# Three more tiles of a channel attention and feed-forward kernel in 16-bit pairs, with stores and scale lines on GpSimd's queue and VectorE's list ordered by due period

## The chip, the cores and the metric

The kernel runs on one core of a Trainium2 chip. The metric is the device time of one execution in microseconds (us), the median of three runs. A core has TensorE (PE; its weight loads are a row of their own, PEld), VectorE (DVE), ScalarE (ACT), GpSimd (POOL) and SyncE (SP), whose queue issues nearly all DMAs here.

## The reference

```python
B, N, C = (4, 6080, 256); d_ff = 2048
qn = q / (norm(q, axis=1) + 1e-6);  kn = k / (norm(k, axis=1) + 1e-6)
s = kn.transpose(0, 2, 1) @ qn / tau            # B x 256 x 256
a = softmax(s, axis=-1)
x = (v @ a).reshape(24320, 256)
h = x @ w_in
g = maximum(0.01 * h, h)
return g @ w_out
```

q, k and v are 32-bit; w_in and w_out arrive as 64-bit floats.

## The kernel before

The attention matrix of a batch is folded into the first weights: for batch b the kernel makes W'[b] = a[b] @ w_in (256 x 2048), and then every token needs only leaky(v @ W') @ w_out. Products are made from pairs: a number is a high and a low part, and high x high, low x high and high x low are added up (`PASSES`). The parts are fp32r (32 bits) in the first batch and 16-bit floats, scaled by powers of two, in the later ones. `T16` is the number of the first tile in 16-bit pairs.

A batch has NT = 6 tiles of tokens, four of 2 x 512 and two of 2 x 496 columns, so there are 24 tiles. A tile takes NPAIR = 8 steps, here called periods, numbered through the run: the fourth tile is periods 24 to 31. In a period TensorE makes the four blocks of h for a pair of feature blocks from seven block products of three matmuls (`block_product`, Strassen's scheme in Winograd's form), and 24 matmuls of the second layer for the period before (`ffn_out`, drawn in portions by `out(n)`). That is 45 matmuls of 512 or 496 columns a period, 360 a tile. Around them ScalarE copies out of PSUM (`taken`) and applies the leaky function (`leaky`), VectorE adds (`add`, three a period) and makes the low halves (the end of `leaky`, four a period).

Everything else hides beside these matmuls, in order of hand-made lists. `at(w, fn)` runs `fn` when period w is built; `put(queue, length, fn)` appends work to a list; at fixed places of each period `slot(queue, room)` takes work from the list's head while it is ready and its nominal lengths fit the room. On VectorE the rooms are 1.45, 2.2, 1.45 and 0.8 us a period from the second tile on. In the first batch that work is: the squares of batch 1's q and k (`square_work`: 47 ScalarE squares with 47 VectorE adds), the sums of w_in's blocks that W' needs (`sums_work`), the splits of the next tile of v (`v_parts`, `v_split_of`), the conversion of w_out into 16-bit pairs (`wo_half`), then the softmax of batch 1 and its W' (`norm_work`, `w_pair`, `w_parts`).

A `Scale` finds the power of two for a 16-bit split: `see` keeps each partition's largest value, `gather` takes their maximum and sends it to a line of DRAM, `read` brings the line back to all partitions, `find` computes the factors. There is one for W', one for w_out and one for each tile of v in 16 bits. All tiles share the SBUF tile `zeros` as the landing place.

W' of a batch lies in DRAM (`w_dram`); `w_load(i, p)` loads a pair's 14 blocks three periods ahead of use into one of four buffers, 896 KB as fp32r and 448 KB as 16-bit. SP's queue issues these loads, the loads of v, q and k, all stores and the lines of scales, in program order.

Of the kernel before, what the change touches and what calls it, by code (L numbers as in the profile page):

```python
# [18 lines left out]
P = 128  # L19
# [17 lines left out]
def channel_attention_ffn(  # L37
# [37 lines left out]
    T16 = NT  # L75
# [51 lines left out]

    class Scale:
# [3 lines left out]
        def __init__(self, name, parts, bufs=1):  # L132
            t = small.tile([P, 16], F32, name=name, bufs=bufs)
            self.most = t[:, 0:parts]
            self.top, self.e, self.up, self.down, self.out = (t[:, x:x + 1] for x in range(8, 13))
            self.line = dram.tile([P, 1], F32, name=name + "_line", bufs=bufs)
            self.seen = 0
# [13 lines left out]
        def read(self):  # L151
            self.all = zeros
            nc.sync.dma_start(out=self.all, in_=self.line.rearrange("p o -> (p o)").partition_broadcast(P))

        def find(self):
            e = self.e.bitcast(I32)
            nc.vector.tensor_reduce(out=self.e, in_=self.all, axis=AX.X, op=ALU.max)
            nc.vector.tensor_scalar(out=e, in0=e, scalar1=0x7F800000, scalar2=None, op0=ALU.bitwise_and)
# [9 lines left out]
            )  # L168

# [3 lines left out]
    class Scores:  # L173


        def __init__(self, b, sizes):
# [5 lines left out]
            self.raw, self.split = {}, {}  # L182
# [4 lines left out]
        def load(self, i, raw):  # L187
# [16 lines left out]
            return last  # L204

# [317 lines left out]

    def win_block(j, h, early):
# [4 lines left out]
        def store():  # L529
            w = win[j, h] = win_new[j, h]  # L530
            stores.append(lambda: nc.sync.dma_start(out=win_dram[j][h], in_=flat(w)))
            if j > 1:
                stores.pop()()
# [13 lines left out]
    def w_tile(i):  # L547
        return work.tile([P, 2, NS, P], pair_type(i), name="w_split", bufs=4)

# [22 lines left out]
    now, w_done, w_stores = [0], {}, []  # L572
# [5 lines left out]
    def w_parts(b, j):  # L578
# [34 lines left out]
        for k in range(2):  # L613
# [9 lines left out]
            def store(x0, n, w=w, p=p):  # L623
                if b:
                    nc.sync.dma_start(
# [12 lines left out]
            def rest(k=k, p=p, blocks=blocks, store=store):  # L638
# [3 lines left out]
                if b == 0:  # L642
                    w = w_split[0, p]
                    w_stores.append(lambda: nc.sync.dma_start(
# [7 lines left out]
    def w_load(i, p):  # L652
        assert (i // NT, p) in w_done
        w = w_tile(i)
        nc.sync.dma_start(
            out=f32(w.rearrange("p x s f -> p (x s f)")), in_=w_dram[i // NT, p].rearrange("p x f -> p (x f)")
        )
# [8 lines left out]

    def wo_region(n):
        return wo[0][:, n * FPB:(n + 1) * FPB, :].rearrange("p f d -> p (f d)")

    def wo_half(n):  # L670

        t, o = None, None
        hi, lo = (wo[x][:, n * FPB:(n + 1) * FPB, :].rearrange("p f d -> p (f d)") for x in range(2))

        def whole():
            nonlocal t, o
            t, o = temp(name="wo_whole"), temp(name="wo16").bitcast(F16)
            return nc.vector.tensor_tensor(out=t, in0=f32(hi), in1=f32(lo), op=ALU.add)

        def low():  # L680
# [3 lines left out]
            nc.sync.dma_start(out=wo16_dram[n], in_=o)  # L684
# [3 lines left out]
        return [  # L688
            ("dve", 0.7, whole),
            ("act", 0.75, lambda: nc.scalar.activation(out=o[:, 0:FPB * C], in_=t, func=AF.Copy, scale=wo_scale.up)),  # L690
            ("dve", 0.8, low),
        ]
# [159 lines left out]
    def ffn_out(i, p):  # L852
# [8 lines left out]
        for name, f, j in (("C11", f1, 0), ("C22", f2, 1), ("C21", f2, 0), ("C12", f1, 1)):  # L861
# [13 lines left out]
            if p == NPAIR - 1 and not early:  # L875
                n0 = b * N + begins[t] + j * n
                act, dve = (nc.scalar.copy, nc.scalar), (nc.vector.tensor_copy, nc.sync)
                parts = [(0, 0, n, act[0], nc.sync), (1, 0, n, *dve)]
                if i == NTILES - 1 and j == 1:
                    parts[1:] = [(1, 0, n // 2, *dve), (1, n // 2, n, *act)]  # L880
# [22 lines left out]
    def at(w, fn, *args):  # L903
        steps.setdefault(w, []).append((fn, args))
# [9 lines left out]

    def put(queue, length, fn, then=(), first=False, ready=lambda: True):


        def run():
            ins = fn()
            for entry in then:  # L920
                if entry[0] == "call":
                    entry[1](*entry[2:])
                else:
                    put(*entry)
# [574 lines left out]
```

## Time and profile before

| what | value |
|---|---|
| median of 3 runs | 2086.39 us (2086.09 to 2086.57) |
| profiled execution | 2086.27 us, its span 2084.2 us |
| PE / PEld busy | 2076.7 us / 1213.5 us |
| DVE / ACT busy | 1600.7 us / 1429.9 us |
| POOL busy | 3.3 us, 11 instructions |
| granted TensorE clock | 1.000 (2.4 GHz) |
| first matmul of the tiles | 85.4 us after the span's start |

The profiled execution took 2.1 us more than its span, the launch and end that no instruction shows. Busy times of different engines overlap. A busy PE row says that a matmul was under way, since matmuls are pipelined, and not how densely they follow each other; that is read from the length of equal stretches of work.

### The profile page before, as it was taken

How to read it: one execution, taken by the hardware profiler on the slowest of the kernel's cores; microseconds unless marked ns; L12 is line 12 of the kernel's file. 1: busy time of each engine (PE TensorE's matmuls, PEld its weight loads, DVE VectorE, ACT ScalarE, POOL GpSimd, SP SyncE). 2: the span in 40 equal slices, each digit the busy share in tenths (PEclk: the TensorE clock that was granted, in tenths of full speed). 3: DMA queues.
4: the chain of work that ended last, by engine and by line, in shares of the span. 5: the costliest groups of instructions: out<-in, count | busy, mean ns of one | idle time of the engine just before them, and what ended most of it. 6: DMA issues, size and time to landing. Idle time of an engine off the chain costs nothing.

```text
span 2084.2 us, 27294 instructions
## 1 busy us (share of the span) xinstructions
PE 2076.7 (100%) x9656; PEld 1213.5 (58%) x9656; DVE 1600.7 (77%) x2905; ACT 1429.9 (69%) x2571; POOL 3.3 (0%) x11
## 2 busy tenths in 40 slices
PE   9999999999999999999999999999999999999999
PEld 8888888888865555544444554554444444444444
DVE  7988888878788778777878787877788767666654
ACT  6577777766577777766667777776666666666665
POOL 0000000000000000000000000000000000000000
PEclk9999999999999999999999999999999999999999
DMA  9946676655543332323533333332343222122120
GB/s 361 397 167 206 201 244 212 171 180 180 185 136 130 106 104 99 104 105 96 175 111 131 115 106 117 104 106 75 120 154 106 83 84 75 66 86 73 66 73 29
DMA packets 120168, 283.47 MB, mean 136 GB/s; under 512 B 15072, under 2 KB 40160, under 8 KB 120032
## 3 DMA queue, kind: packets, MB, share of 16 engines
q1 hardware_dynamic: 119664, 281.41, 40.2%
q8 instruction: 76, 1.25, 0.3%
q14 instruction: 60, 0.49, 0.1%
q10 hardware_dynamic: 368, 0.32, 0.1%
HBM read 227.93 MB, written 53.75 MB: 135 GB/s over the span
## 4 chain that ended last, share of the span: by engine, by line
PE 98%; DVE 1%; DMA 1%; ACT 0%; issue 0%; SPq 0%; ACTq 0%; DVEq 0%
PE ps_o L867 48%; PE ps_x L811 24%; PE ps_z L811 16%; PE ps_s L253 3%; PE ps_y L811 2%; PE ps_y L253 2%; PE ps_s L1060 1%; PE ps_o L253 1%; DMA qk_raw<-in_k_dram 1%; PE ps_y L558 0%; PE ps_y L1060 0%; DVE sq_acc L210 0%; PE ps_z L558 0%; SPq L201 0%; ACT sq L209 0%
## 5 line engine op out<-in xcount | busy, mean ns | idle before, releaser
L867 PE MATMUL ps_o<-g_split,w_out_split 128*128 128x512 f16 (+3 forms) x4608 | 1123.3, 380 | 0.0
L834 DVE TENSOR_TENSOR g_split<-g,g_split 128x512 f16<-128x512 f32 (+3 forms) x768 | 525.0, 684 | 208.3 <-ACT g_split L824 201.1
L811 PE MATMUL ps_x<-v_split,w_split 128*128 128x512 f16 (+3 forms) x2280 | 620.3, 381 | 0.1
L867 PEld LDWEIGHTS <-w_out_split 128*128 128x128 f16 x3456 | 338.2, 98 | 400.0
L824 ACT ACTIVATE g<-h 128x512 f32<-128x512 f32 (+1 forms) x576 | 360.4, 626 | 281.7 <-DVE h L841 279.0
L841 DVE TENSOR_TENSOR h<-ps_z,h 128x512 f32<-128x512 f32 (+1 forms) x520 | 354.7, 682 | 234.0 <-ACT h L847 225.9
L847 ACT COPY h<-ps_x 128x512 f32<-128x512 f32 (+1 forms) x576 | 331.5, 575 | 292.8 <-PE ps_x L811 291.6
L811 PEld LDWEIGHTS <-w_split 128*128 128x128 f16 x3024 | 288.8, 98 | 342.2 <-issue 11.9
L811 PE MATMUL ps_z<-v_split,w_split 128*128 128x512 f16 (+3 forms) x1560 | 423.0, 380 | 1.4 <-DVE h L841 1.4
L824 ACT ACTIVATE g_split<-h 128x512 f16<-128x512 f32 (+3 forms) x576 | 351.4, 610 | 0.0
L867 PEld LDWEIGHTS ps_o<-g_split,w_out_split 128*128 128x128 f32 x1152 | 216.4, 188 | 43.5
L830 ACT CAST g_split<-g 128x512 f16<-128x512 f32 (+3 forms) x192 | 118.0, 615 | 5.9
L811 PEld LDWEIGHTS ps_x<-v_split,w_split 128*128 128x128 f32 x576 | 107.7, 188 | 22.4 <-ACT h L847 0.4
L824 ACT ACTIVATE g<-ps_x 128x512 f32<-128x512 f32 (+1 forms) x192 | 113.1, 589 | 9.7 <-PE ps_x L811 7.4
L764 DVE SCALAR_TENSOR_TENSOR v_split<-v_raw,v_scale,v_split 128x512 f16<-128x512 f32 (+1 forms) x125 | 93.2, 745 | 4.4
L223 DVE TENSOR_TENSOR sq_acc<-sq_acc,sq 128x512 f32<-128x512 f32 x141 | 96.3, 683 | 0.2
L220 ACT ACTIVATE sq<-qk_raw 128x512 f32<-128x512 f32 x141 | 87.5, 630 | 0.0
L811 PEld LDWEIGHTS ps_z<-v_split,w_split 128*128 128x128 f32 x408 | 76.2, 188 | 16.7 <-DVE h L841 1.4
L253 PE MATMUL ps_s<-qk_split 128*128 128x512 f32 x192 | 73.2, 391 | 0.0
L232 DVE TENSOR_TENSOR qk_split<-qk_raw,qk_split 128x512 fp32r<-128x512 f32 x96 | 65.6, 683 | 0.0
L785 DVE TENSOR_TENSOR v_raw<-v_raw 128x512 f32<-128x512 f32 (+1 forms) x94 | 64.0, 681 | 1.4
L253 PE MATMUL ps_y<-qk_split 128*128 128x512 f32 x192 | 60.3, 336 | 0.0
(163 smaller groups left out, 1128.1 us busy)
## 6 DMA issues: line engine op xcount, KB each, us to landing
w_split<-w_dram SPq DMA_DIRECT2D x144, 448.0 KB, 3.8
w_split<-w_dram SPq DMA_DIRECT2D x40, 896.0 KB, 5.0
qk_raw<-in_q_dram SPq DMA_DIRECT2D x115, 256.0 KB, 4.8
qk_raw<-in_k_dram SPq DMA_DIRECT2D x115, 256.0 KB, 5.1
v_raw<-in_vT_dram SPq DMA_DIRECT2D x32, 512.0 KB, 4.7
out_dram<-o_sb SPq DMA_DIRECT2D x64, 256.0 KB, 3.1
win<-win_dram SPq DMA_DIRECT2D x26, 512.0 KB, 3.7
win<-win_sums SPq DMA_DIRECT2D x24, 512.0 KB, 3.5
```

Source lines behind the costliest of these rows:

```text
L220: return nc.scalar.activation(out=out, in_=self.chunk(j), func=AF.Square)
L223: return nc.vector.tensor_tensor(out=self.acc[0], in0=self.acc[0], in1=sq, op=ALU.add)
L232: return nc.vector.tensor_tensor(out=sp[:, :, 1, :], in0=self.chunk(j), in1=f32(sp[:, :, 0, :]), op=ALU.subtract)
L253: mm = nc.tensor.matmul(out=out, lhsT=lhsT, rhs=rhs, start=start, stop=stop, skip_group_check=True)
L764: return nc.vector.scalar_tensor_tensor(out=sp[:, 1, 0:w], in0=src, scalar=up, in1=sp[:, 0, 0:w], op0=ALU.mult, op1=ALU.subtract)
L811: mm = nc.tensor.matmul(out=ps[:, 0:n], lhsT=w[:, x, a, :], rhs=sp[:, y, 0:n], start=first and k == 0, stop=k == 2, skip_group_check=True,)
L824: return nc.scalar.activation(out=to, in_=h[:, 0:n], func=AF.Prelu, alpha=0.01, scale=G_SCALE if i >= T16 else 1.0)
L830: issued["act"] = nc.scalar.copy(out=sp[:, 0, 0:n], in_=out[:, 0:n])
L834: issued["dve"] = nc.vector.tensor_tensor(out=sp[:, 1, 0:n], in0=out[:, 0:n], in1=f32(sp[:, 0, 0:n]), op=ALU.subtract)
L841: issued["dve"] = nc.vector.tensor_tensor(out=h[:, 0:n], in0=ps[:, 0:n], in1=h[:, 0:n], op=ALU.add)
L847: issued["act"] = nc.scalar.copy(out=h[:, 0:n], in_=ps[:, 0:n])
L867: issued["pe"] = nc.tensor.matmul(out=o_ps[i][j][h][:, 0:n], lhsT=wo_lhsT(i, x, f, h), rhs=sp[:, y, 0:n], start=p == 0 and early and k == ...
```

## The change

`T16` becomes 3: the fourth, fifth and sixth tile of the first batch (i = 3, 4, 5) run in 16-bit pairs too. What they need is made earlier, or newly made:

- W' of batch 0 is needed in 16 bits as well. `w16_work(p)` loads the high half of a pair from `w_dram` (SP), lets a DMA on GpSimd's queue add the low half onto it in SBUF (`pair_sum`), splits the sum on VectorE (`high`, two `low`) and stores it to `w16_dram` (GpSimd's queue): eight times in a chain, due by periods 18 to 25. `w_load` of tiles 3 to 5 reads `w16_dram`.
- The scale of W' comes from w_in at the start: ScalarE sums squares (`w_seen`, eight) where VectorE took maxima in `sums_work`; `roots` takes the root of the power of two. The scale of w_out comes from eight ScalarE sums in periods 8 and 9 where VectorE took maxima in periods 13 to 20.
- w_out's conversion, periods 24 to 31 before, is a chain `wo_go` due by periods 20 to 26, its loads follow in periods 22 to 28 (before 43 to 49).
- Tiles 3 to 5 of v get a `Scale` each.

The line of a scale is stored and read back on GpSimd's queue without a period between, and `find` stands ready 1.75 periods after `gather` (`past`). Stores of W', of the sums, of w_out's 16-bit form and of the output move from SP's to GpSimd's queue, but for the last of the run. Work on a list carries a due period (`wanted`); `slot` takes the ready piece with the earliest due (none counts as three periods from now) in place of the head. Batch 1's squares start at period 10 (before 8), with at most three groups of q and k held in SBUF.

```diff
-    T16 = NT
+    T16 = 3
...
         def gather(self):
             last = nc.vector.tensor_reduce(out=self.top, in_=self.most, axis=AX.X, op=ALU.max)
-            nc.sync.dma_start(out=self.line, in_=self.top)
-            at(now[0] + 1, self.read)
+            last = nc.vector.tensor_scalar(
+                out=self.top, in0=self.top, scalar1=2.0**126, scalar2=None, op0=ALU.min
+            )
+            nc.gpsimd.dma_start(out=self.line, in_=self.top)
...
+            self.all, self.landed = zeros, past(1.75)
+            nc.gpsimd.dma_start(out=self.all, in_=self.line.rearrange("p o -> (p o)").partition_broadcast(P))
...
+    def summed(values, to, func):
+        unread = temp(name="unread").bitcast(F16)[:, 0:values.shape[-1]]
+        return nc.scalar.activation(out=unread, in_=values, func=func, accum_out=to)
...
+    def w16_work(p):
+        n = NS * P // 2
+        xs = [slice(x * n, (x + 1) * n) for x in range(2)]
+        t = work.tile([P, NS * P], F32, name="w_whole", tag="qk_split", bufs=3)
+        pair_sum(t, w_dram[0, p][:, 0, :], w_dram[0, p][:, 1, :], nc.sync)
+        def high():
+            nonlocal o
+            o = work.tile([P, 2, NS * P], F16, name="w16", tag="qk_split", bufs=3)
+            ins = nc.vector.tensor_scalar(out=o[:, 0, :], in0=t, scalar1=w_scale.up, scalar2=None, op0=ALU.mult)
+            if p + 1 < NPAIR:
+                w16_work(p + 1)
+            return ins
+        def low(x):
+            ins = nc.vector.scalar_tensor_tensor(
+                out=o[:, 1, xs[x]], in0=t[:, xs[x]], scalar=w_scale.up, in1=o[:, 0, xs[x]],
+                op0=ALU.mult, op1=ALU.subtract,
+            )
+            if x:
+                nc.gpsimd.dma_start(
+                    out=w16_dram[p].rearrange("p x f -> p (x f)"), in_=o.rearrange("p x f -> p (x f)")
+                )
+                w16_done[p] = now[0]
+            return ins
+        there = past(1.25)
+        landed = lambda: there() and (p == 0 or p - 1 in w16_done) and w_scale.landed() and w_scale not in in_zeros
+        with wanted(TL + p + 2):
+            at(now[0] + 1, put, "dve", 0.6, high, [
+                ("dve", 0.75, lambda: low(0), [("dve", 0.75, lambda: low(1), (), True)], True)
+            ], True, landed)
...
-        w = w_tile(i)
-        nc.sync.dma_start(
-            out=f32(w.rearrange("p x s f -> p (x s f)")), in_=w_dram[i // NT, p].rearrange("p x f -> p (x f)")
-        )
+        w, src = w_tile(i), w_dram[i // NT, p]
+        if T16 <= i < NT:
+            assert p in w16_done
+            src = w16_dram[p]
+        nc.sync.dma_start(out=f32(w.rearrange("p x s f -> p (x s f)")), in_=src.rearrange("p x f -> p (x f)"))
...
+    def pair_sum(out, high, low, queue):
+        queue.dma_start(out=out, in_=high)
+        return nc.gpsimd.dma_start(out=out, in_=low, accum_op=ALU.add)
...
     def slot(queue, room):
         engine = queue.split("_")[0]
-        while todo[queue] and todo[queue][0][0] <= room and todo[queue][0][1].ready():
-            length, fn = todo[queue].popleft()
+        if queue == "dve":
+            clock[0] += 0.25
+        while True:
+            order = sorted(range(len(todo[queue])), key=lambda n: todo[queue][n][1].due or now[0] + 3)
+            for n in order:
+                length, fn = todo[queue][n]
+                if fn.ready() and (length <= room or fn.due is None):
+                    break
+            else:
+                return
+            if length > room:
+                return
+            del todo[queue][n]
             room -= length
             with in_order(engine):
                 ins = fn()
             issued[engine] = ins
+
+    def past(periods):
+        until = clock[0] + periods
+        return lambda: clock[0] >= until
...
-        begin_at, span = (NPAIR, 20) if b == 1 else (0, 28)
+        begin_at, span = (NPAIR + 2, 19) if b == 1 else (0, 28)
...
+    for j in range(2):
+        for h in range(CH):
+            run("act", w_seen, j, h, f32(win[j, h][:, 0, :]))
     run("pe", sc.norms_mm)
```

## Rows read from the trace of the kernel before

**Rows 1.** The page: busy time by engine, and the ending chain's shares by engine

```profile
PE 2076.7 (100%) x9656; PEld 1213.5 (58%) x9656; DVE 1600.7 (77%) x2905; ACT 1429.9 (69%) x2571; POOL 3.3 (0%) x11
...
PE 98%; DVE 1%; DMA 1%; ACT 0%; issue 0%; SPq 0%; ACTq 0%; DVEq 0%
```

**Rows 2.** Windows, one a tile: length, busy PE, PEld, DVE, ACT, POOL, clock, DMA, GB/s

```profile
178.50:260.60 82.10, 81.86 (x361) 67.46 (x360) 68.43 (x110) 64.61 (x116) 0.00 (x0) 1.00 0.63 212
260.60:342.20 81.60, 81.60 (x361) 67.54 (x360) 71.89 (x117) 62.83 (x113) 0.00 (x0) 1.00 0.64 220
342.20:425.30 83.10, 83.10 (x373) 68.72 (x372) 69.09 (x133) 60.44 (x111) 0.52 (x1) 1.00 0.63 188
425.30:510.90 85.60, 85.60 (x387) 71.76 (x387) 66.04 (x129) 55.57 (x102) 0.00 (x0) 1.00 0.51 171
510.90:596.10 85.20, 85.20 (x383) 71.46 (x382) 67.00 (x135) 51.97 (x95) 0.00 (x0) 1.00 0.58 192
...
942.30:1024.60 82.30, 81.66 (x390) 39.61 (x389) 62.67 (x125) 53.56 (x102) 0.00 (x0) 1.00 0.39 124
1024.60:1104.90 80.30, 80.30 (x382) 38.63 (x381) 67.08 (x140) 50.80 (x96) 0.00 (x0) 1.00 0.46 146
...
1691.20:1768.90 77.70, 77.70 (x362) 35.24 (x361) 52.00 (x88) 50.35 (x91) 0.00 (x0) 1.00 0.23 76
```

**Rows 3.** Groups by line, VectorE, 178.5 to 425.3 us: busy, mean ns | idle before

```profile
L834 DVE TENSOR_TENSOR g_split<-g,g_split 128x512 fp32r<-128x512 f32 x97 | 67.0, 691 | 13.9 <-ACT g_split L824 13.3
L841 DVE TENSOR_TENSOR h<-ps_z,h 128x512 f32<-128x512 f32 x72 | 49.7, 690 | 21.9 <-ACT h L847 18.5 <-PE ps_z L811 3.1
...
L141 DVE TENSOR_REDUCE w_scale<-win 128x1 f32<-128x512 f32 x8 | 5.4, 678 | 0.0
L141 DVE TENSOR_REDUCE wo_scale<-w_out_split 128x1 f32<-128x512 f32 x8 | 5.4, 676 | 0.0
L681 DVE SCALAR_TENSOR_TENSOR wo<-wo_whole,wo_scale,wo 128x512 f16<-128x512 f32 x6 | 4.5, 746 | 0.0
L678 DVE TENSOR_TENSOR wo_whole<-w_out_split 128x512 f32<-128x512 f32 x6 | 4.1, 682 | 0.0
```

**Rows 4.** Groups by line, ScalarE: a square in 178.5 to 425.3 us, an accumulator's read

```profile
L220 ACT ACTIVATE sq<-qk_raw 128x512 f32<-128x512 f32 x47 | 28.2, 629 | 0.0
...
L374 ACT ACTIVATION_READ_ACCUMULATOR s_sb<-s_sb,nm 128x1 f32 x8 | 1.5, 187 | 0.0
```

**Rows 5.** Groups by line and shape, VectorE, whole run

```profile
L764 DVE SCALAR_TENSOR_TENSOR v_split<-v_raw,v_scale,v_split 128x512 f16<-128x512 f32 x83 | 62.4, 751 | 3.0
L762 DVE TENSOR_SCALAR v_split<-v_raw,v_scale 128x512 f16<-128x512 f32 x83 | 39.8, 479 | 0.0
...
L773 DVE TENSOR_TENSOR v_split<-v_raw,v_split 128x512 fp32r<-128x512 f32 x27 | 18.3, 690 | 0.7
...
L769 DVE CAST v_split<-v_raw 128x512 fp32r<-128x512 f32 x20 | 8.4, 418 | 0.0
```

**Rows 6.** Tiles v_scale_line and zeros: ns min/median/max, first and last start us

```profile
L147 SPq DMA_DIRECT2D v_scale_line<-v_scale x18: 319/326/327, 530.1 to 1939.8; - x18
...
L157 DVE TENSOR_REDUCE v_scale<-zeros x18: 274/275/277, 546.6 to 1954.8; 128x1 f32<-128x128 f32 x18
```

**Rows 7.** Windows of two single periods, columns as in rows 2

```profile
95.90:107.70 11.80, 11.80 (x52) 9.69 (x52) 11.76 (x29) 9.77 (x18) 0.00 (x0) 1.00 0.90 349
...
565.90:576.00 10.10, 10.10 (x47) 8.50 (x46) 9.95 (x22) 6.24 (x12) 0.00 (x0) 1.00 0.32 93
```

**Rows 8.** Timeline of ScalarE ahead of the first tile: start, duration, [idle before]

```profile
47.51 0.62 ACT L483 CAST win_early<-f_x 128x512 fp32r<-128x512 f32 x1 [2.38 <-DVE f_x L477]
...
59.16 0.72 ACT L465 ACTIVATE f_scale<-f_scale,exp_bias 128x512 int32<-128x512 int32 x1 [7.33 <-DVE f_scale L459]
```

**Rows 9.** DMA issues: count, KB each, median us from issue to landing

```profile
w_split<-w_dram SPq DMA_DIRECT2D x144, 448.0 KB, 3.8
w_split<-w_dram SPq DMA_DIRECT2D x40, 896.0 KB, 5.0
...
zeros<-v_scale_line SPq DMA_DIRECT2D x18, 64.0 KB, 5.4
...
v_scale_line<-v_scale SPq DMA_DIRECT2D x18, 0.5 KB, 7.5
```

More of the change, by code (lines that the diff above doesn't have):

```diff
@@ L204, in load, with here @@
             return last
+        def here(self, j):
+            return self.since.get(self.of[j][0], now[0]) < now[0]
         def group_squares(self, i, sq):
@@ L570, in w_taken @@
         return ins
-    now, w_done, w_stores = [0], {}, []
+    now, clock, w_done, w_stores = [0], [0], {}, []
     def w_stored():
@@ L683, in low @@
             )
-            nc.sync.dma_start(out=wo16_dram[n], in_=o)
+            nc.gpsimd.dma_start(out=wo16_dram[n], in_=o)
             wo16_done.add(n)
             return ins
[L688 to L692, printed above, removed]
+        return [("dve", 0.7, begin), ("act", 0.6, high), ("dve", 0.75, low)]
     wo16_done = set()
@@ L913, in slot @@
             issued[engine] = ins
+    def past(periods):
+        until = clock[0] + periods
+        return lambda: clock[0] >= until
     def put(queue, length, fn, then=(), first=False, ready=lambda: True):
         def run():
[L919 to L924, printed above, removed]
+            with wanted(run.due):
+                ins = fn()
+                for entry in then:
+                    if entry[0] == "call":
+                        entry[1](*entry[2:])
+                    else:
+                        put(*entry)
             return ins
-        run.ready = ready
+        run.ready, run.due = ready, due[0]
         (todo[queue].appendleft if first else todo[queue].append)((length, run))
@@ L936, in acc_tile, with loads @@
         return work.tile([P, 2, C], F32, name="sq_acc", bufs=1)
-    cast_ahead = []
+    cast_ahead, sq_ahead = [], []
+    raw_held, raw_wanted = [0], deque()
+    def loads():
+        while raw_wanted and raw_held[0] < 3:
+            raw_held[0] += 1
+            sc, i = raw_wanted.popleft()
+            sc.since[i] = now[0]
+            sc.load(i, qk_raw())
     def chunk_work(sc, j):
@@ L1089, in split @@
                     then = [("call", w_pair, b, q + 1)]
-                put("dve", *part, then)
+                with wanted(WPB + 2 * j + max(0, n - 2) // 2 - 4 if b == 1 else None):
+                    put("dve", *part, then)
         def half_done():
@@ L1107, in w_pair @@
         load(1)
-        step(0)
+        with wanted(WPB - 2 * NPAIR if b == 1 else None):
+            step(0)
     FIRST = (2, 0, 1, 3, 4, 5)
@@ L1201, in channel_attention_ffn @@
         for j in range(NCHUNK):
-            at(when[j], square_work if b == 1 else chunk_work, sc, j)
+            with wanted(when[j] + 2 if b == 1 else None):
+                at(when[j], square_work if b == 1 else chunk_work, sc, j)
         e = w0 + begin_at + span + 1
-        at(e, norm_work, sc)
-    for pair in range(NWC // 2):
-        at(9 + 8 * pair, sums_work, pair)
+        with wanted(e if b == 1 else None):
+            at(e, norm_work, sc)
+    with wanted(33):
+        at(10, sums_work, 0)
@@ L1207, in channel_attention_ffn, with wo_go @@
     wo_n = NF // FPB
[L1208 to L1217 removed]
+    def wo_go(n):
+        if n < wo_n:
+            with wanted(TL + n // 2 * 2 + 4):
+                put_steps([*wo_half(n), ("call", wo_go, n + 1)], True)
@@ new lines, in channel_attention_ffn @@
+    TL = (T16 - 1) * NPAIR
+    with wanted(NPAIR + 2):
+        for n in range(wo_n):
+            at(NPAIR + n // 4, put, "act", 0.65, lambda n=n: summed(
+                f32(wo_region(n)), wo_scale.most[:, n:n + 1], AF.Abs
+            ))
+    at(NPAIR - 1, put, "dve", 0.2, w_scale.gather)
+    at(NPAIR, put, "dve", 1.2, lambda: w_scale.find(True), (), True, lambda: w_scale.landed())
+    at(NPAIR + 4, put, "dve", 0.2, wo_scale.gather)
+    at(NPAIR + 4, put, "dve", 0.6, wo_scale.find, [("dve", 0.3, weights_down), ("call", wo_go, 0)], True,
+       lambda: wo_scale.landed())
@@ L1409, in channel_attention_ffn @@
                 todo[name + "_next"].clear()
-            for fn, args in steps.get(i * NPAIR + p, ()):
-                fn(*args)
+            for fn, args, by in steps.get(i * NPAIR + p, ()):
+                with wanted(by):
+                    fn(*args)
+            loads()
             if p:
```

162 lines of the change are left out of this document (103 added, 59 removed).

## Prediction

> **What bounds the kernel now.** I read the page first: TensorE is busy for the whole span and the chain that ended last lies on it for 98% [rows 1]. So nothing but fewer or denser matmuls shortens the run, and any other work costs only where it makes TensorE wait. Next I read windows cut at the tiles' first matmuls [rows 2]. All have 360 matmuls of the two layers; the count behind PE shows what was added (small ones of the softmax, and 21 of W' in the fifth and sixth tile). The third tile, in fp32r pairs, takes 81.6 us with one matmul beyond; the 20th, in 16-bit pairs of the same width, 77.7. That is 0.227 against 0.216 us a matmul at the same granted clock of 1.00, and PEld is busy for 67.5 us in the one and 35.2 in the other. The denser stream is what the change can win. VectorE's groups over tiles two to four say how near the next engine is [rows 2, 3]: 209.4 us busy of 246.8 (85%), and of the 37.4 idle ones 35.8 stand ahead of the additions and the low halves, where it waits mostly for ScalarE.
>
> **What the 16-bit tiles save.** Fourth tile: 81.6 - 77.7 = 3.9 us; its own 83.1 holds the softmax's small matmuls, which stay. Sixth tile: 85.2 against 80.3 in the 12th, the same 496 columns with the same 21 matmuls of W': 4.9 us. Fifth: 85.6 against 82.3 in the 11th: 3.3 us; but that tile has three matmuls more and 0.64 us of idle TensorE, so up to 4.9 is possible and I take 3.8. Sum 12.6 us, between 12.1 and 13.7 [rows 2]. The pair of comparisons with W' in it covers the mixing of fp32r and 16-bit matmuls too.
>
> **What VectorE gets and loses in tiles two to four** (periods 8 to 31, the stretch where it is fullest):
> - Out: 16 maxima of 0.68 us, -10.8 [rows 3]. They become 16 ScalarE sums, each a square with an accumulator's read, 0.63 + 0.19 = 0.82 us [rows 4]; four of them lie ahead of the first tile, four in it and eight (6.6 us) in tile two, whose ScalarE is busy for 64.6 of 82.1 [rows 2]. It has the room.
> - In: `w16_work`. No row has 896 columns, so I scale up the 512-column forms: 0.48 x 1.75 = 0.84 for `high`, 0.75 x 0.875 = 0.66 for each `low`, 2.15 a pair, 17.2 for eight [rows 5]. If a part of each time is fixed it is less; upward I see nothing.
> - In: two of the eight pieces of `wo_half`, which stood behind period 31 (six are counted in this stretch): 2 x (0.68 + 0.75) = 2.9 [rows 3].
> - In: scales and 16-bit splits for tiles four and five of v, made a tile ahead. Four maxima are 2.7; seven splits cost 0.751 + 0.479 in place of 0.690 + 0.418, so 0.9 [rows 5]; the small operations of `gather` and `find` are about seven, 0.28 for the largest [rows 6], taken as 1.2. That is 4.8 a tile, 9.6 for two. The sixth tile's falls into the fifth, which has 19 us to spare [rows 2].
> - In: finding W's scale, which came later before, with the five small operations of `roots`: about 2.
> - Batch 1's 47 additions start two periods later and still end inside; of the softmax some may slide out of the stretch, uncounted.
>
> Sum: 209.4 - 10.8 + 17.2 + 2.9 + 9.6 + 2 = 230.3 us, in 82.1 + 81.6 + 79.2 = 242.9: 95%, where it was 85%. A mean period has 9.6 us of VectorE against 10.2 in fp32r and 9.7 in 16 bits. Does TensorE bear that? In single periods it does: 11.76 of 11.80 us in period 1 and 9.95 of 10.10 in period 45, neither longer for it [rows 7]. The waits ahead of the additions shrink when VectorE comes later, since its data is then there. But the list can overfill: the rooms sum to 5.9 us and the seven fixed operations to 4.8, 10.7 against 9.7. I take four or five periods of the fourth tile as overfull by some 0.45 us, 2.0 us of TensorE's time; bounds 0 and the 11 of the first rival.
>
> **The other edits.** In the ramp ScalarE gets 3.3 us of sums between 47.5 and 59.2 us, where it idles for most of the time [rows 8], but two copies of v's splits stand behind them, on which VectorE's way to the softmax waits: 0.3 us, between 0 and 1. Moving stores to GpSimd's queue frees SP's; no transfer on SP is on the ending chain, so nothing is gained. What is queued behind a waiting GpSimd instruction are only other stores, accumulations and lines: TensorE feels them through VectorE, by the second and third rival. The order by due dates changes nothing in the number of operations; in the later batches most work has none, so the order stays nearly as it was, and no chance of a gain is in it since TensorE has almost no idle time there. Loads of W' fall to half for three tiles, 5.0 to 3.8 us [rows 9], but they are three periods ahead, so nothing. The additional traffic, 8 x 1.34 MB over some 160 us, is 67 GB/s on top of 212 to 220 at a share of 0.63 [rows 2]: room for it.
>
> **The sum**, from the profiled execution's 2086.27 us (0.12 below the median): 2086.3 - 12.6 + 2.0 + 0.3 = 2076.0 us, 0.50% less. About 0.2%, 4.2 us, is what can be told from no change here. The likeliest case's own range is 2072.6 (13.7 saved, nothing lost) to 2079.
>
> **Rivals.**
> 1. VectorE becomes the bound in tiles two to four. If its waits don't shrink below those of the third tile, 81.6 - 71.9 = 9.7 us each [rows 2], the three need 230.3 + 29 = 259 of 242.9 us: TensorE waits 16 us and the time is 2086.3 - 12.6 + 16 + 0.3 = 2090. With half of them left it is 245, 2 us over, my sum. Against it speak the two full periods [rows 7]; for it, that those are single ones, and that no stretch of 24 periods at 95% is to be seen. Chance 0.22, 2079 to 2091, the middle at 2085.
> 2. The other side: W's pairs come late. `high` stands ready 1.25 periods, 12.7 us, after the chain's last step. In that time SP's load has to land (3.8 us) and GpSimd's accumulation after it. No accumulation and no DMA of GpSimd is in the trace. From below it is like a 448 KB load, 3.8 us, in all 7.9; from above I take one that reads and writes at half speed twice over, four times 3.8, in all 19.3 with the issues. A late landing stops VectorE in order: behind `high` stand the additions and low halves that TensorE's next product needs. TensorE bears about 1.0 us of it: between the block that an addition empties and the next product into that bank lie eight matmuls, 1.7 us, less 0.69 for the addition itself [rows 3]. So eight waits cost 8 x (19.3 - 12.7 - 1.0) = 45 us at worst: 2121. It turns the sign from a wait of 1.0 + 10.3/8 = 2.3 us on, so an accumulation of 10.9 us. SP issues the load up to a period ahead of VectorE, which makes it milder. I take a value near 6 us, since a 896 KB load lands in 5.0 [rows 9] and accumulation moves as many bytes in. Chance that it costs over 8 us: 0.11, 2084 to 2106.
> 3. The lines of scales come late on GpSimd's queue. On SP store and read take 7.5 + 5.4 us to land [rows 9], 13.5 with the issues of 0.33; from the store to `find` it was 16.5 us in the first case and 15.0 in the last, and VectorE did not wait [rows 6]. Now 1.75 periods are 17.0 us (16.5 in narrow tiles). So GpSimd may take 3 us longer, and 4 before TensorE feels it; then each us costs 21 (one a tile from the fourth on). At 0.5 us over it is 10 us, 2086; at 1.0, 21 us, 2097, slower. Nothing in the trace prices GpSimd's issue; 11 instructions of 3.3 us are all it did [rows 1]. Chance 0.08.
>    The Trainium skill, SBUF — State Buffer (SBUF: two separate sides), says that GpSimd can't write its DMAs' descriptors while VectorE runs an operation in a mode that takes both ports, and gives about 620 ns alone and about 3100 ns beside such a copy. By that page a store and a read would be an estimated 5.0 us longer together, past the 4 that TensorE bears, and the time would be this rival's. Here the operations of 0.42 and 0.48 us for 512 columns would be of that kind [rows 5]; they are short and 14 a tile, so I hold it for the exception. No run shows it so far.
> 4. The change doesn't do what it says: the fourth to sixth tile get no denser, say because W's and v's loads wait. Then it is 2086 + 2 = 2088. The tiles of later batches with the same code speak against it [rows 2]. Chance 0.02.
>
> **How the numbers follow.** The forecast has 0.57. Faster by over 0.2% (below 2082.2): the forecast, half of the first rival's lower part (0.09), 0.03 each of the second's and third's mildest: 0.72. Within 0.2%: 0.08 of the first, 0.02 of the third, 0.02 of the fourth: 0.12. Slower: 0.05 of the first, 0.08 of the second, 0.03 of the third: 0.16. The range is 2072 to 2088: below lies 0.02, above 0.17 or so.
>
> **What would show it.** Windows of the fourth to sixth tile near 79 to 80, 81 to 82 and 80.3 us, with PEld at about 40 in place of 70; VectorE at some 95% in tiles three and four with waits ahead of L841's and L834's successors shrunk below 10 us a tile; TensorE's gaps, if any, in periods 16 to 31 behind additions. If rival two holds, VectorE's idle time stands ahead of the 896-column `high`, eight times; if three, ahead of the reduction of `zeros`, in every tile to the end, in the later batches too. The first tile of the run should start within 1 us of 85.4. The prediction is wrong if the tiles behind period 48 get longer at all, since I count nothing there.

## The result, and the profile after

The changed kernel takes 2098.83 us (median of four runs, 2097.84 to 2100.01) beside 2086.24 us of the kernel before (2086.06 to 2086.57): 1.006 times as long, 95% interval 1.0043 to 1.0078. It is slower by 12.6 us where 10.4 less were forecast. The profiled execution took 2097.84 us, its span is 2096.0 us, 11.8 more than before.

The page's busy times and its chain, to be read beside [rows 1]:

```profile
PE 2070.7 (99%) x9656; PEld 1117.7 (53%) x9656; DVE 1617.7 (77%) x2974; ACT 1436.5 (69%) x2603; POOL 137.9 (7%) x239
...
PE 88%; DVE 7%; DMA 2%; ACT 2%; issue 1%; SPq 0%; POOL 0%; DVEq 0%; POOLq 0%; ACTq 0%
```

TensorE's busy time fell by 6.0 us, and the weight loads by 96: the denser stream is there. But the chain, which lay on TensorE for 98%, now lies there for 88%. Windows cut at the first matmuls of the second to sixth tile, columns as in [rows 2]:

```profile
178.30:267.10 88.80, 84.23 (x361) 68.42 (x360) 68.81 (x128) 66.58 (x128) 9.18 (x15) 0.98 0.75 212
267.10:357.90 90.80, 84.94 (x362) 68.34 (x361) 76.77 (x130) 62.20 (x114) 10.28 (x17) 0.96 0.79 232
357.90:440.00 82.10, 79.61 (x370) 38.04 (x370) 73.69 (x140) 59.78 (x110) 8.89 (x16) 1.00 0.67 198
440.00:522.30 82.30, 81.67 (x391) 39.61 (x390) 68.10 (x133) 55.56 (x106) 7.46 (x13) 1.00 0.57 166
522.30:602.60 80.30, 80.30 (x383) 38.62 (x382) 66.54 (x138) 50.81 (x94) 9.46 (x15) 1.00 0.52 147
```

The fourth to sixth tile are shorter by 1.0, 3.3 and 4.9 us. The loss stands ahead of them: the second tile, still in fp32r, takes 88.8 us in place of 82.1, the third 90.8 in place of 81.6, and in both the granted clock is below 1.00. VectorE is not full in them (77% and 85%), and PE is idle for 4.6 and 5.9 us.

I cut the run further, at the first matmul of each period (the 21st, 42nd, ... of the first layer). Two periods of 10.20 us before carry most of it, 14 (15.87) and 19 (17.61). Waits in these two, first 240.5 to 256.4, then 299.5 to 317.2 us (us in total, times, longest):

```profile
DVE w L598 <- DMA w_whole<-w_dram: 6.0, 1, 6.0
PE ps_z L890 <- DVE h L920: 4.3, 1, 4.3
...
DVE w L598 <- DMA w_whole<-w_dram: 5.7, 1, 5.7
PE ps_z L890 <- DVE h L920: 5.2, 1, 5.2
```

`w L598` is the 896-column `high` of a pair of W'. The chain that ended last within 240 to 257 us shows the way of the delay (start, length, what):

```profile
235.74 8.24 DMA w_whole<-w_dram
...
244.53 7.16 DMA w_whole<-w_dram
...
251.79 0.17 DVE w L598
...
252.39 0.69 DVE h L920
...
253.13 0.96 PE ps_z L890 x3
```

SP's load of the high half lands after 8.24 us, then GpSimd's accumulation after 7.16, then VectorE gets to `high`, one addition, and TensorE's next product. TensorE's gap is 4.33 us, and the price is not over with it. Windows of the 3.4 and the 6.8 us that follow the two gaps:

```profile
254.10:257.50 3.40, 3.40 (x9) 2.63 (x9) 3.38 (x6) 2.41 (x5) 0.58 (x1) 0.50 0.85 136
305.30:312.10 6.80, 4.12 (x10) 3.24 (x11) 5.30 (x13) 2.67 (x5) 0.00 (x0) 0.50 0.91 339
```

The granted clock is 0.50 there, 1.2 GHz; before and after it is 1.00. Half of 3.40 us of matmuls is 1.7 us lost: 4.3 + 1.7 = 6.0 of the 6.25 by which periods 14 and 15 are longer. In period 19 it is 5.2 + 4.12 / 2 = 7.3 of 7.4.

The rest, against the kernel before: periods 16 to 18 are 1.7 us longer and period 24 is 1.9 longer than without the accumulations (first experiment); from period 48 to the first matmul of the last period 3.1 us come up (2075.2 - 602.6 beside 2065.6 - 596.1), most of it in periods 49, 97 and 145 (+1.3, +1.1, +0.55); the last period with the end of the run takes 20.73 in place of 18.57, 2.2 us. With the saving, which the first experiment shows undisturbed as 11.1: -11.1 + 6.2 + 7.4 + 1.7 + 1.9 + 3.1 + 2.2 = 11.4 of 11.8 us.

Why was one `high` of eight late by 6.0 us, another by 5.7, and six not? The rows of the landing tile:

```profile
L742 SPq DMA_DIRECT2D w_whole<-w_dram x8: 319/327/669, 112.0 to 354.5; - x8
L743 POOL DMA_DIRECT2D w_whole<-w_dram x8: 867/886/897, 116.0 to 359.3; - x8
...
  DVE w L598: 11.7, 2
DMA to landing us min/median/max: 3.3/5.6/10.0
```

Those are SP's eight loads, GpSimd's eight accumulations and the wait. A transfer of the sixteen takes 3.3 to 10.0 us to land. In the fifth pair it was 9.97 for the load and 9.16 for the accumulation. The DMA view of 285 to 300 us, in 40 slices of 0.375 us, shows that load, issued at 286.27:

```profile
DMA  6997669990000547992406352458999998999999
GB/s 161 355 273 257 246 80 172 48 96 0 0 10 29 57 67 96 57 57 19 19 0 29 29 19 57 76 162 344 335 382 421 440 415 350 374 410 382 367 380 269
...
v_scale_line<-v_scale POOLq DMA_DIRECT2D x1, 0.5 KB, 8.1
```

From the eighth slice to the 26th, for 7 us, it is 0 to 96 GB/s, though SP has the pair's load, from 287.71 another load of W' and from 291.24 two of q and k under way; from the 28th slice on it is over 330, but for the last. What is under way beside them is the store of a scale's line, 128 values of 4 bytes, issued on GpSimd's queue at 285.39 and landed at 293.46 us.

### The profile page after: what moved, and what is told of

It reads as the page before. It is cut to its first block, busy times and chain, and to the rows that moved or that the text cites. A ratio compares the mean times of both kernels' runs of the same rounds, so it can differ in the third digit from the quotient of the medians.

```text
span 2096.0 us, 27456 instructions
## 1 busy us (share of the span) xinstructions
PE 2070.7 (99%) x9656; PEld 1117.7 (53%) x9656; DVE 1617.7 (77%) x2974; ACT 1436.5 (69%) x2603; POOL 137.9 (7%) x239
## 4 chain that ended last, share of the span: by engine, by line
PE 88%; DVE 7%; DMA 2%; ACT 2%; issue 1%; SPq 0%; POOL 0%; DVEq 0%; POOLq 0%; ACTq 0%
PE ps_o L946 42%; PE ps_x L890 21%; PE ps_z L890 14%; PE ps_s L281 4%; PE ps_o L281 2%; DVE h L920 2%; PE ps_y L890 2%; DMA w_whole<-w_dram 2%; DVE g_split L913 2%; PE ps_y L281 2%; PE ps_s L1182 1%; ACT g L903 1%; ACT g_split L903 1%; DVE v_split L843 1%; DMA qk_raw<-in_k_dram 0%
## 5 line engine op out<-in xcount | busy, mean ns | idle before, releaser
L946 PE MATMUL ps_o<-g_split,w_out_split 128*128 128x512 f16 (+2 forms) x4608 | 1118.3, 379 | 0.0
L913 DVE TENSOR_TENSOR g_split<-g,g_split 128x512 f16<-128x512 f32 (+2 forms) x768 | 524.5, 683 | 204.1 <-ACT g_split L903 196.7
L946 PEld LDWEIGHTS <-w_out_split 128*128 128x128 f16 x4032 | 394.5, 98 | 465.5
L890 PE MATMUL ps_x<-v_split,w_split 128*128 128x512 f16 (+2 forms) x2280 | 617.9, 380 | 1.3 <-ACT h L926 1.1
L890 PE MATMUL ps_z<-v_split,w_split 128*128 128x512 f16 (+2 forms) x1560 | 421.6, 379 | 14.3 <-DVE h L920 14.1
L903 ACT ACTIVATE g_split<-h 128x512 f16<-128x512 f32 (+2 forms) x576 | 351.1, 610 | 0.0
L946 PEld LDWEIGHTS ps_o<-g_split,w_out_split 128*128 128x128 f32 x576 | 109.4, 190 | 23.6
L909 ACT CAST g_split<-g 128x512 f16<-128x512 f32 (+2 forms) x192 | 117.9, 614 | 5.9
L841 DVE TENSOR_SCALAR v_split<-v_raw,v_scale 128x512 f16<-128x512 f32 (+1 forms) x146 | 69.5, 476 | 0.0
L890 PEld LDWEIGHTS ps_x<-v_split,w_split 128*128 128x128 f32 x288 | 54.4, 190 | 13.3 <-ACT h L926 1.8
```

The costliest lines, as they stand in the source:

```text
L841: nc.vector.tensor_scalar(out=sp[:, 0, 0:w], in0=src, scalar1=up, scalar2=None, op0=ALU.mult)
L890: mm = nc.tensor.matmul(out=ps[:, 0:n], lhsT=w[:, x, a, :], rhs=sp[:, y, 0:n], start=first and k == 0, stop=k == 2, skip_group_check=True,)
L903: return nc.scalar.activation(out=to, in_=h[:, 0:n], func=AF.Prelu, alpha=0.01, scale=G_SCALE if i >= T16 else 1.0)
L909: issued["act"] = nc.scalar.copy(out=sp[:, 0, 0:n], in_=out[:, 0:n])
L913: issued["dve"] = nc.vector.tensor_tensor(out=sp[:, 1, 0:n], in0=out[:, 0:n], in1=f32(sp[:, 0, 0:n]), op=ALU.subtract)
L946: issued["pe"] = nc.tensor.matmul(out=o_ps[i][j][h][:, 0:n], lhsT=wo_lhsT(i, x, f, h), rhs=sp[:, y, 0:n], start=p == 0 and early and k == ...
```

## The experiments

Each kernel is the changed one with the edit shown. Ratios are against the kernel before on the same chip (2086.3 to 2086.5 us).

**1. No accumulation.** The low half of W' of batch 0 is left out of the sum in `pair_sum`.

```diff
-        queue.dma_start(out=out, in_=high)
-        return nc.gpsimd.dma_start(out=out, in_=low, accum_op=ALU.add)
+        return queue.dma_start(out=out, in_=high)
```

> Leaves out the accumulation: W' of the fourth to sixth tile is made from the high halves alone, without GpSimd's eight DMAs. Theory (two late accumulations stop VectorE in periods 14 and 19, and TensorE behind it): those two periods go back to near 10.2 us, the clock stays at 1.00, 14 us fewer: 2085. Rival (VectorE's list is simply overfull and the stalls come out wherever it is): less than 5 us gained, other periods of 14 to 28 grow: above 2093.

2083.55 us (2082.46 to 2086.07), ratio 0.9988 (0.9978 to 0.9997). Windows of the same five tiles:

```profile
178.30:260.90 82.60, 82.36 (x362) 67.35 (x361) 68.91 (x128) 66.82 (x127) 6.44 (x12) 1.00 0.74 211
260.90:344.20 83.30, 82.56 (x361) 66.97 (x359) 76.61 (x130) 62.02 (x114) 8.07 (x15) 1.00 0.73 235
344.20:424.30 80.10, 79.37 (x369) 37.94 (x369) 73.74 (x140) 59.79 (x111) 7.43 (x14) 1.00 0.65 199
424.30:506.60 82.30, 81.66 (x390) 39.62 (x389) 68.14 (x133) 55.53 (x106) 7.43 (x13) 1.00 0.58 166
506.60:587.00 80.40, 80.40 (x382) 38.64 (x381) 66.63 (x138) 50.78 (x95) 9.44 (x15) 1.00 0.52 147
```

Periods 14 and 19 are 10.20 us again and the clock stays at 1.00. 15.3 us of the loss hang on this one DMA. Period 14 lies in the second tile and 19 in the third; VectorE is busy there for 68.8 and 76.8 us with the accumulations and for 68.9 and 76.6 without, so its load isn't what the two periods paid for. The saving undisturbed is 3.0 + 3.3 + 4.8 = 11.1 us against [rows 2].

**2. `high` ready three quarters of a period later.** The accumulations stay.

```diff
-        there = past(1.25)
+        there = past(2.0)
```

> The split of a pair of W' stands ready 2.0 periods after its loads are issued instead of 1.25; nothing else changes. Theory (the accumulations are late, by some 6 us at worst): VectorE waits for none, 13 us fewer: 2086. Rival (a slower chain only moves the lateness on, to the loads of W' of the fourth tile in periods 24 to 28): TensorE stalls there instead, 2093 or more.

2085.82 us (2083.29 to 2088.61), ratio 0.9998 (0.9989 to 1.0008). Periods 14 and 19 are 10.2 us, so in these two lateness against the place on VectorE, not the work, was the cost. Periods 16 and 17 are 10.2 us here too, but they stay at 11.2 and 10.5 in the first experiment, where nothing is late: there it counts in which period VectorE gets the work. And period 18 takes 14.4. Its wait:

```profile
ACT sq L248 <- DMA out_dram<-o_sb: 4.3, 1, 4.3
```

ScalarE's square takes over the buffer of an output whose store on GpSimd's queue is not down yet. VectorE's and TensorE's waits behind it bring the granted clock to 0.50 again, from 292.0 to 295.4 us.

**3. All stores and lines back on SP's queue**, only the accumulations stay on GpSimd's. Every edited line reads like

```diff
-            nc.gpsimd.dma_start(out=self.line, in_=self.top)
+            nc.sync.dma_start(out=self.line, in_=self.top)
```

> Every store and every line of a scale back on SP's queue; GpSimd's queue issues the eight accumulations alone. Theory (an accumulation is late through its own load and transfer, not through what stands ahead of it on GpSimd's queue): the stalls of periods 14 and 19 stay, only the end of the run gets 1 to 2 us shorter: 2097. Rival (queueing on GpSimd delays the accumulations): the stalls go, 2085.

2098.40 us (2096.24 to 2100.62), ratio 1.0059 (1.0044 to 1.0074): nothing won. Period 14 is even longer (18.1), 19 is shorter (11.9), and period 9 takes 18.4, since ScalarE waits 6.9 us there for an output's store. So in period 14 the queue that issues is not the cause. In period 19 it has a part: the pair's load takes 3.4 us here, the accumulation, beside the line's store, 11.4, and 5.7 of the 7.4 us are gone.

**4. The list from its head, and the end on SP**, from period 48 on.

```diff
+                if i == NTILES - 1:
+                    parts = [(*x[:4], nc.sync if x[4] is nc.gpsimd else x[4]) for x in parts]
...
+            if now[0] >= WPB:
+                order = range(min(1, len(todo[queue])))
```

> From period 48 on the lists are taken from the head only, as before the change, and the last tile's stores go out on SP's queue. Theory (the sorted list lets squares overtake casts and fills VectorE in periods 48 and 96; GpSimd's last stores and its drain lengthen the end): periods 49, 97 and 145 lose 1.3, 1.1 and 0.6 us, the end 2.2: 2094. Rival (GpSimd's DMAs slow VectorE or the transfers everywhere): only the end shortens, by under 1.5 us: 2097 or more.

2099.87 us (2099.57 to 2100.5), ratio 1.0067 (1.005 to 1.0084). A miss: periods 49 and 97 come down half way (10.48), but 96 and 144 grow to 10.0 us, 145 does not come down, and the end is 20.0 us. From period 48 to the last period's first matmul it takes 1472.4 us, 0.2 less than with the changed kernel. Windows of period 96 of the kernel before, then of this one:

```profile
1104.90:1114.50 9.60, 9.60 (x47) 4.41 (x46) 8.43 (x20) 6.47 (x12) 0.00 (x0) 1.00 0.53 171
```

```profile
1114.90:1124.90 10.00, 9.86 (x47) 4.39 (x46) 9.86 (x26) 6.73 (x13) 3.11 (x5) 1.00 0.37 124
```

VectorE still has 26 operations in place of 20 there, though the list is taken from its head. So taking a piece from behind the head is not by itself what costs these 3 us.

**5. A plain second load** over the first in place of the accumulation, so that the low half alone is split; the two transfers stay one behind the other.

```diff
-        return nc.gpsimd.dma_start(out=out, in_=low, accum_op=ALU.add)
+        return nc.gpsimd.dma_start(out=out, in_=low)
```

> GpSimd's second DMA of a pair of W' copies the low half over the high one instead of adding it: the same bytes at the same place in the same chain, with no addition (W' of the fourth to sixth tile is then made from the low halves alone). Theory A (two transfers one after the other, each 6 to 9 us long in this traffic, don't fit 12.7 us): the stalls of periods 14 and 19 stay, 2096 to 2099. Theory B (the adding itself is what takes long): the second transfer lands in under 5 us and the stalls go, 2084.

2097.48 us (2091.36 to 2098.28), ratio 1.0046 (1.0031 to 1.0061). Windows of its periods 14 and 19:

```profile
240.50:256.90 16.40, 12.33 (x47) 9.74 (x47) 9.71 (x22) 8.90 (x16) 1.65 (x3) 0.83 0.78 278
300.00:317.30 17.30, 13.07 (x47) 10.28 (x47) 10.18 (x21) 8.61 (x16) 1.80 (x4) 0.80 0.90 297
```

The two periods stall as before. Adding is not the cause; that a second transfer has to follow the first is, since without it (first experiment) the stalls go. A plain second load lands in 3.7 to 7.8 us, the accumulation in 5.2 to 9.2.

**6. Outputs on SP, `high` at 2.0**: the second experiment with the outputs' stores back on SP.

```diff
+        there = past(2.0)
...
+                act, dve = (nc.scalar.copy, nc.scalar), (nc.vector.tensor_copy, nc.sync)
+                parts = [(0, 0, n, act[0], nc.sync), (1, 0, n, *dve)]
```

> As x2_there_2, and all stores of the output on SP's queue again. In x2 ScalarE waited 4.3 us in period 18 for a buffer whose store on GpSimd's queue had not landed. Theory (GpSimd's queue, with accumulations and stores of W' ahead, keeps output stores back): that stall of 4.2 us goes and the end shortens by 1 to 2: 2080. Rival (any queue is late there, as the DMA engines are full): the stall stays or turns up on SP: 2084 or more.

2086.85 us (2085.68 to 2089.65), ratio 1.0005 (0.9995 to 1.0014). Period 18 still takes 14.5 us: the output's store is late on either queue. What it shares with the other transfers is the DMA engines, and a line's store is among these. In experiments 2, 6, 7 and 10 the tile's last output store is issued 4 to 5 us ahead of the line's and lands only 0.1 to 1.7 us ahead of it, after 14 to 17 us (second experiment: 274.0 to 290.5 us, the line 278.7 to 290.6); in the changed kernel, where the line comes later, it takes 5.2. That the line holds it up too is likely, but no run took the line away there.

**7. `high` at 1.75 periods, the last tile's stores as before the change.**

```diff
+        there = past(1.75)
...
+                if i == NTILES - 1:
+                    parts = [(*x[:4], nc.sync if x[4] is nc.gpsimd or n < 2 else x[4]) for n, x in enumerate(parts)]
```

> The split of W' stands ready 1.75 periods after its loads' issue, and the last tile's output stores are as before the change. Theory (the waits were up to 7 us over 1.25 periods; 1.75 is 5 us more): at most one short wait is left, 2083, and the last period goes from 20.7 to 18.6 us. Rival (what is late is late by what the list does, so that any such number only moves the stall): 2090.

2084.29 us (2081.81 to 2088.02), ratio 0.9993 (0.9984 to 1.0003). Half a period cures periods 14 and 19; 18 takes 10.75 here. The last period is 19.9 us, 1.3 over the kernel before. It varies: by one trace of each kernel, with the changed kernel's end it is 19.9 to 20.7 in five (the changed one, experiments 1, 2, 5 and 9), with the last stores on other queues 18.6 to 20.0 in six (3, 4, 6, 7, 8, 10), 1.0 us less in the mean. The last store is issued 15.64 us after the last period's first matmul both before and after the change. It then takes 3.4 us to land in each of the five kernels and 2.0 to 2.8 in the six, 2.0 in the kernel before. From that landing to the end of the span it is 0.9 to 1.9 us, with either end.

**8. Nominal lengths of W' pieces near their real ones, from batch 1 on**, and the same end.

```diff
-            yield 1.0, begin
-            yield 1.2, rest
+            yield (1.2 if b else 1.0), begin
+            yield (1.45 if b else 1.2), rest
```

> The two kinds of splits of W' of later batches stand on the list with 1.2 and 1.45 us in place of 1.0 and 1.2 (they take 1.3 to 1.5), and the last tile's stores are as before the change; the accumulations stay late. Theory (VectorE is overfull in periods 48 and 96 because the list, no longer stopped by its head, fits in more than nominal lengths say): periods 49, 97 and 145 shorten by 1 us each, the end by 2, so 2094. Rival (the additions there are late for another reason): only the end gains, 2097.

2095.42 us (2092.81 to 2097.18), ratio 1.0041 (1.0026 to 1.0056). From period 48 to the last period's first matmul it takes 1469.3 us, as before the change (1469.5), and not 1472.6. Windows of periods 48 and 49 of the changed kernel, then of this one:

```profile
602.60:612.50 9.90, 9.76 (x46) 4.37 (x45) 9.76 (x25) 7.69 (x15) 3.03 (x5) 1.00 0.36 123
612.50:623.50 11.00, 10.02 (x47) 4.39 (x45) 10.03 (x19) 8.83 (x18) 2.47 (x5) 1.00 0.45 150
```

```profile
605.60:615.20 9.60, 9.60 (x47) 4.43 (x46) 8.27 (x20) 7.70 (x15) 2.11 (x4) 1.00 0.41 123
615.20:625.40 10.20, 9.84 (x46) 4.37 (x45) 10.06 (x21) 7.54 (x14) 2.83 (x5) 1.00 0.56 191
```

The pieces are counted as 1.0 and 1.2 us, and their operations' rows add up to 1.28 and 1.50. With the true lengths five operations fewer fall into period 48, VectorE is no longer full there, and the 3 us are gone. So the lengths overfill the period. Why they do so after the change and did not before is not shown: experiment 4 speaks against the list's order.

**9. No lines.** A line's store and its read back are left out, and each partition's own largest value stands in for that of all.

```diff
-            nc.gpsimd.dma_start(out=self.line, in_=self.top)
...
-            self.all, self.landed = zeros, past(1.75)
-            nc.gpsimd.dma_start(out=self.all, in_=self.line.rearrange("p o -> (p o)").partition_broadcast(P))
+            self.all, self.landed = self.top, past(1.75)
```

> Leaves out the exchange between partitions: no line of a scale is stored or read back, each partition takes its own largest value. In the changed kernel's trace no packet but those of the pair's load moves from 287 to 294 us, while a line of 128 four-byte values is being stored, and the same stands around the store in the kernel before. Theory (a line's store holds up all transfers for 6 us; in period 19 a pair of W' is caught in it, in period 14 plain traffic is enough): period 19 goes from 17.6 to near 10.2 us, period 14 keeps its 5 us: 2089 to 2092. Rival (the hold-up is the traffic's own): both stalls stay, 2097 or more.

2089.68 us (2088.96 to 2091.81), ratio 1.0018 (1.0009 to 1.0027). Windows of periods 14 and 19:

```profile
241.00:256.80 15.80, 11.98 (x47) 9.46 (x46) 9.25 (x22) 8.64 (x16) 2.34 (x3) 0.89 0.76 212
299.30:309.50 10.20, 10.20 (x46) 8.45 (x45) 9.74 (x21) 8.33 (x16) 1.56 (x3) 1.00 0.88 298
```

Period 19 is whole, period 14 stays. The fifth pair's load, issued at 286.48, lands after 3.2 us where it took 10.0 with the line's store ahead of it. So the line is the cause in period 19 and not in period 14. In period 14 the DMA view of 235.5 to 252 us of the changed kernel shows plain traffic:

```profile
DMA  3039999993599999999999999899999999998210
GB/s 35 17 156 434 417 410 330 325 129 70 184 395 461 439 417 417 395 425 473 395 402 437 434 400 492 333 400 387 390 256 202 199 196 226 304 365 348 96 61 26
...
w_split<-w_dram SPq DMA_DIRECT2D x1, 896.0 KB, 7.6
win_sums<-win_t POOLq DMA_DIRECT2D x1, 512.0 KB, 9.8
w_dram<-w POOLq DMA_DIRECT2D x1, 448.0 KB, 7.2
```

The engines are 90% busy or more in most slices, at 390 to 490 GB/s in half of them, with nine transfers of 256 to 896 KB. The third pair's load and accumulation wait among them. That this traffic makes them late is read from the view; no run took it away.

**10. The three cures together**: 1.75 periods, the lengths of experiment 8, the end of 7.

> The split of W' ready at 1.75 periods, the true lengths of W's splits on the list (1.2 and 1.45 us), the last tile's output stores as before the change. Theory (the three causes are apart, so what x7 and x8 gained adds up): x7 less 3.3 us in periods 49 to 145: 2081, 0.26% below the kernel before. Rival (chance of landing: another of the eight pairs gets caught): 2084 to 2088, no different from before.

2079.55 us (2077.66 to 2082.51), ratio 0.9971 (0.9959 to 0.9983): faster than both kernels, by 6.7 us than the one before and by 19 than the changed one. Windows of the third and the fourth tile:

```profile
261.00:345.40 84.40, 82.31 (x361) 67.04 (x359) 75.88 (x129) 62.08 (x114) 11.18 (x18) 1.00 0.86 258
345.40:425.70 80.30, 79.29 (x370) 37.99 (x370) 73.64 (x140) 59.94 (x111) 9.32 (x16) 1.00 0.62 192
```

2.8 us of the third tile over [rows 2] are left, in two periods: in 18 the square waits 3.2 us for an output's store, and in 23 one of VectorE's additions waits 2.3 us for ScalarE.

## Why the prediction was wrong

- **The step that failed: the price of a pair of W' in the second rival.** The mechanism stood there, with its row to look for, and had 0.11, 2084 to 2106, in which the measured time lies; the sum that gave 2076 had no term for it. I took SP's load as 3.8 us and the accumulation as near 6, below the 12.7 that stand between one `high` and the next. The accumulation was about right (5.2 to 9.2 us). The load was not: 8.2 and 10.0 us in the two late pairs, since 3.8 is the median of a row over the whole run [rows 9], and these ran, one in a stretch of full DMA engines, the other behind a line's store. "Room for it", which I read from a tile's mean share of 0.63, says nothing of the 15 us in which a load, a store of W', one of the sums and q and k meet. From the `high` before to the landing it took 18.6 us in the third pair (233.1 to 251.69) and 20.9 in the fifth (285.0 to 305.9), around the 19.3 that I had as the upper bound for all eight. In the third, 2.6 us of it passed before SP issued the load, since it stood behind loads of q and k that waited for a ScalarE square; I had SP issue it ahead of VectorE. A sum of eight equal waits was also the wrong form: six pairs waited for nothing, and two cost nearly everything.
- **What a wait costs TensorE.** I took TensorE to bear 1.0 us of a wait of VectorE. The gaps were 4.3 and 5.2 us for waits of 6.0 and 5.7, so that term held; the half clock behind each gap, 1.7 and 2.1 us, was not in it.
- **The saving.** 11.1 us of 12.6. The fifth tile gave 3.3 where I had moved towards the upper end (3.8): four small matmuls of the softmax slid into it from the fourth (391 in place of 387). The sixth gave 4.8 of 4.9. The fourth gave 3.0 of 3.9, since its period 24 still makes the 24 matmuls of the second layer for the third tile, in fp32r (10.16 us in the first experiment, beside 9.71 of period 26), and period 25 is 1.1 us longer than the 26th: TensorE waits 0.7 us there for ScalarE's copy `h`, which stands behind a square and two copies of the third tile's output.
- **VectorE's sum** was too high, though not to the harm of the forecast. `w16_work` took 16.2 us of 17.2 predicted, but tiles two to four hold 219.3 us (68.8 + 76.8 + 73.7) where 230.3 were forecast: half of the sums of w_in's blocks (7.4 us) and some of the softmax slid behind period 31. The low halves and additions wait less, as said, 26.3 us in place of 35.8. Groups of VectorE, 178.3 to 440.0 us, beside [rows 3]:

```profile
L920 DVE TENSOR_TENSOR h<-ps_z,h 128x512 f32<-128x512 f32 x72 | 49.4, 686 | 14.6 <-ACT h L926 12.1 <-PE ps_z L890 2.3
L913 DVE TENSOR_TENSOR g_split<-g,g_split 128x512 fp32r<-128x512 f32 x67 | 46.1, 689 | 7.8 <-ACT g_split L903 7.4
...
L604 DVE SCALAR_TENSOR_TENSOR w<-w_whole,w_scale,w 128x448 f16<-128x448 f32 x16 | 10.7, 679 | 0.0
L598 DVE TENSOR_SCALAR w<-w_whole,w_scale 128x896 f16<-128x896 f32 x8 | 5.5, 681 | 11.7 <-DMA w_whole<-w_dram 11.7
```

  The first rival came in a mild form, 1.3 us in periods 16 and 17 (VectorE is busy for 10.4 us of the 10.55 of period 17), near the 2.0 of the forecast though in other periods. The ramp cost nothing (first tile at 85.0 us).
- **"Behind period 48 nothing" was wrong** by 3.1 us and 2.2 at the end. I saw that the new order has no due dates to act on there, and took the order of VectorE's work to stay nearly as it was. It did not: more splits of W' fall into periods 48, 96 and 144 (20 operations of VectorE before, 24 to 25 after). Experiment 8 shows that their nominal lengths let this happen; why it began with the change stays open. Of the end, 1.4 us are the landing of the last store, 3.4 us in place of 2.0, and most of that goes with the last stores on GpSimd's queue (experiment 7); the rest lies between that landing and the end of the span and varies from kernel to kernel.
- **Stores on GpSimd's queue are covered by VectorE, "nothing gained".** Their issue costs nothing that I can find (experiment 3), but what is late is not only what I listed: ScalarE waits for an output's store through a shared buffer, with a square in experiments 2, 6, 7 and 10 and with a copy in experiment 3. In period 24 ScalarE waits 2.4 us at `wo L761` for the store of the piece before, and TensorE 1.7 for the copy behind it.
- **The third rival did not come.** VectorE waited 0.2 us for a line in the whole run. The rule of the Trainium skill, SBUF — State Buffer (SBUF: two separate sides), which stood beside it, would show as issues of about 3.1 us; GpSimd's 228 issues take 0.53 to 1.17 us here, in a run in which VectorE is busy for 77%, so no run shows that rule at work. The line did its harm as a store that holds up others, which neither rival had. In the kernel before, SP waited for the line to land before it issued the read back and all that stood behind it (of SP's waits there):

```profile
SPq L153 <- DMA v_scale_line<-v_scale: 128.9, 18, 7.9
```

  So none of the 144 loads of W' for batches 1 to 3 was issued there while a line was being stored. From GpSimd's queue the line no longer keeps SP's transfers out of its way: 17 of the 144 are.

Open: why more splits fall into periods 48, 96 and 144 after the change, and whether period 18's late output store is the line's doing too.

## What to carry to other kernels

A transfer's median over the run says little about a chain of transfers in the busiest stretch: take the slow end of the row for each link, add the links, and give the consumer's place in its engine's order that much slack. Half a period more was worth 14 us here. Make the nominal lengths of a list's pieces true before the list is changed: errors that cost nothing before cost 3 us here afterwards. A store of 4 bytes a partition held up every load of W' beside it, so look at what will be under way beside a transfer that is moved to another queue. And a store is a wait for whoever takes over its buffer, on whichever queue it goes.

## What the runs showed of the hardware

- While a line of 128 values of 4 bytes was stored, the other transfers nearly stood still. Two windows after the change:

```profile
229.00:235.00 6.00, 6.00 (x28) 4.99 (x27) 5.79 (x10) 5.36 (x11) 0.23 (x1) 1.00 0.89 39
287.50:294.00 6.50, 6.50 (x30) 5.39 (x29) 6.27 (x12) 5.84 (x12) 0.00 (x0) 1.00 0.84 40
```

  The last two columns are the DMA share and GB/s: 39 and 40 where the tiles' means are 147 to 232, with a load of W' under way in both. A share of 0.84 at 40 GB/s means packets that are under way and do not end: from 288 to 293 us single packets of 3584 bytes took up to 6.8 us, where 0.14 is the median. It is so to the end of the run: of the 144 loads of W' (448 KB) for batches 1 to 3, 17 were issued while a line was being stored, and they took 9.0 to 11.7 us; the other 127 took 3.0 to 6.6, with a median of 3.5. Without lines (experiment 9) the median of all 144 is 3.5. The kernel before can't show it, since from 2.6 us behind the issue of such a line on nothing else was under way there.
- An accumulating DMA's 128 packets of 3584 bytes took 291 ns in the median, plain ones of that size 140. The plain second loads of experiment 5 moved the same bytes in 64 packets of 7168 bytes, 272 ns in the median.
- The Trainium skill, DMA: Bandwidth & Descriptors (Anatomy of one DMA), fits a transfer of GpSimd's by 2.0 us plus its bytes at 436 GB/s. For 448 KB an estimate from it is 3.1 us; the plain second loads of experiment 5 took 3.7 to 7.8, so under this traffic the fit is a lower bound and the measured rows decide.
- After gaps of 4.3 and 5.2 us TensorE's granted clock was 0.50 for 3.4 and 6.8 us.
